# Attention with memory and a gated feed-forward: first statistics, last inverses and last adds moved between engines

## The chip, the cores and the metric

The kernel runs on one core of a Trainium2 chip. The metric is device time in microseconds from the launch to the end of the program on that core. The kernel before takes 261.97 us (median of 3 runs, 261.74 to 262.56). Its profiled execution spans 260.2 us from the first instruction to the last; all times inside the kernel below are counted from the start of that span.

The engines go by short names in the profile: PE is TensorE (matmul), PEld its weight load, DVE is VectorE, ACT is ScalarE, POOL is GpSimd, SP is SyncE, which here only issues transfers.

## The reference

The input is 2048 rows of 448 numbers in bfloat16. The rows are normalised, and then go through two branches, whose results are multiplied and added to the input. Cut to what matters:

```python
xn = layernorm(x)                       # (x - mean) / sqrt(var + 1e-5)
# branch A: 16 heads of 28, four segments of 512 rows
for s in range(4):
    p = softmax(q_s @ k_s.T * scale + causal_mask)
    a_dot = p @ v_s
    a_mem = (phi(q_s) @ M) / (phi(q_s) @ z + 1e-6)
    o_s = g * a_mem + (1 - g) * a_dot   # g = sigmoid(beta), one per head
    M, z = M + phi(k_s).T @ v_s, z + phi(k_s).sum(rows)
A = concat(o) @ wo
# branch B
B = (gelu(xn @ w_gate) * (xn @ w_up)) @ w_down
out = x + A * silu(B)
```

## The kernel before

A segment is 512 rows in NB = 4 blocks of 128; the 16 heads stand in G = 4 groups of HG = 4 heads, each head padded from 28 to 32 columns, so that a group fills 128 partitions. Column 28 of each padded head of v holds ones, so the softmax denominators come out of the same matmuls as the products. Attention of a segment is ten steps, and all other work (projections, down projections, memory reads, inverses, output projections) is placed between those steps by one table of step numbers.

The start: block statistics are shared between VectorE (blocks 0 and 1) and ScalarE (blocks 2 and 3).

```python
for i in range(44):                                     # L116: keeps TensorE busy while x loads
    nc.tensor.matmul(out=idle[:, 0:P], lhsT=wz[:], rhs=wz[:], start=True, stop=True)
w_dma(nc.sync, wv_sb, A_wv)
w_dma(nc.scalar, wk_raw, A_wk)
w_dma(nc.sync, wq_raw, A_wq)
...
def stats(b):                                           # L288 to L295, VectorE and a power on GpSimd
    nc.vector.bn_stats(out=st[:], in_=xs[:, b, :])
    nc.vector.bn_aggr(out=mv[:, b, :], in_=st[:])
    ... # rstd = (var + EPS) ** -0.5; tensor_scalar on vector, pow on gpsimd
def scale_x(b):                                         # L301, L304
    nc.vector.tensor_scalar(out=xn[b][:, 0:D], ...)     # (x - mean) * rstd
    nc.vector.tensor_scalar(out=xn[b][:, D:], ...)      # last 64 columns once more
def turn(b, copy=nc.scalar.copy):                       # L315, L316: four transposes, one copy out
    for c in range(NDC):
        nc.tensor.transpose(tp[:, c, :], xn[b][:, c * P:(c + 1) * P], ident[:])
    copy(out=dst, in_=tp[:])
def stats_scalar(b):                                    # L321 to L323
    nc.scalar.activation(out=junk[:], in_=xs[:, b, :], func=ACT.Copy, accum_out=mv[:, b, 0:1])
    nc.scalar.activation(out=mv[:, b, 0:1], in_=mv[:, b, 0:1], func=ACT.Copy, scale=-1.0 / D)
    nc.scalar.activation(out=junk[:], in_=xs[:, b, :], func=ACT.Square, bias=mv[:, b, 0:1],
                         accum_out=mv[:, b, 1:2])

def layer_norm_first():
    ...
    for b in (2, 3): stats_scalar(b)
    for b in (0, 1): stats(b)
    for b in (2, 3): power_scalar(b)                    # L329, L331 on gpsimd
    more_loads()                                        # w_gate, w_up, beta, next x, w_down: all on sync
    for b in (0, 1): scale_x(b)
    turn(0, nc.vector.tensor_copy)
    turn(1)
    for b in (2, 3): scale_x(b)
    pad_weight("wk")                                    # L144, vector
    for i in range(2):                                  # L358, L359
        nc.gpsimd.memset(vaug[i][:, :, :, Dh:HP], 0.0)
        nc.gpsimd.memset(vaug[i][:, :, :, Dh:Dh + 1], 1.0)
    for b in range(NB):
        run(units0[8 + b:9 + b])                        # value projection of a block, L431, L433
        if b < 2: turn(b + 2)
    pad_weight("wq")                                    # L144, scalar
# then eight projections of keys and queries (L392), then the first gate phase
```

GpSimd fills `spread`, the matrix that spreads inverses over partitions, with one memset and three affine selects (L188, L191); these wait for nothing.

The end: the denominators of the attention product go by DMA to a tile with 64 numbers in a row (`dc`), are inverted there, split into three bfloat16 terms, and go by DMA to `rows`; a matmul with `spread` brings them to all partitions. The last group of the last segment takes another way, by float32 matmuls:

```python
def invert(s, side, g0=0, g1=G, ...):                   # L541 to L549
    nc.vector.tensor_scalar(out=d, in0=d, ...)          # add 1e-6 or 0, times gate
    nc.vector.reciprocal(out=d, in_=d)
    for i in range(3):
        eng.tensor_copy(out=t[p, i, :], in_=d)
        if i < 2: eng.tensor_tensor(out=d, in0=d, in1=t[p, i, :], op=ALU.subtract)
        queues[i].dma_start(out=rows[...], in_=t[p, i, :])
def inverses(s, side, g, at):                           # L560
    nc.tensor.matmul(out=r[:], lhsT=spread[:, g, :], rhs=rows[at][:], start=True, stop=True)
def invert_last():                                      # L571 to L580
    for b in range(NB):
        nc.tensor.matmul(out=d[:, b, :], lhsT=o_a[:, b * P:(b + 1) * P], rhs=pick[:], ...)
    nc.vector.reciprocal(out=lden[:], in_=d[:])
    for h in range(2):
        nc.vector.tensor_tensor(out=linv[...], in0=lden[...], in1=lgate[...], op=ALU.mult)
def combine_last():                                     # L586 to L590
    for b in range(NB):
        nc.tensor.matmul(out=r[:, b * P:(b + 1) * P], lhsT=linv[:, b, :], rhs=unit[:], ...)
    for h in range(2):
        nc.vector.tensor_tensor(out=oT[3][:, G - 1, c], in0=o_a[:, c], in1=r[:, c], op=ALU.mult)
def combine(s, g, at=0):                                # L613, L614
    nc.vector.tensor_tensor(out=o_a, in0=o_a, in1=r, op=ALU.mult)
    add.tensor_tensor(out=dst, in0=o_a, in1=oU.pop((s, g, 1)), op=ALU.add)
...
combine_last()
srcs = [(om[0], G - 1)] + [(oT[3][:, g, :], g) for g in range(G)]     # memory part of group 3 apart
for b, a, z in ((0, 0, G), (1, 0, G), (0, G, G + 1), (1, G, G + 1), (2, 0, G + 1), (3, 0, G + 1)):
    for n in range(a, z): ...                           # L921: output matmuls, block by block
for b in range(NB):
    nc.vector.tensor_tensor(out=t, in0=t, in1=acc[...], op=ALU.mult)            # L926
    add = nc.gpsimd if b < 3 else nc.vector
    add.tensor_tensor(out=o_out[:, b, :], in0=t, in1=xr[3][:, b, :], op=ALU.add) # L928
    (nc.scalar if b % 2 else nc.sync).dma_start(out=o_v[3][:, b, :], ...)
```

In the same stretch stand the last down projections (L653 on TensorE, L659 on ScalarE, L663 on VectorE) and the output projections of segment 2 (L688, L691, L696).

Of the kernel before, what the change touches and what calls it, by code (L numbers as in the profile page):

```python
# [48 lines left out]
def fast_path(tc, A_x, A_wq, A_wk, A_wv, A_wo, A_beta, B_w_gate, B_w_up, B_w_down, out):  # L49
# [16 lines left out]
    with ExitStack() as ctx:  # L66
# [49 lines left out]
        for i in range(44):  # L116
            nc.tensor.matmul(out=idle[:, 0:P], lhsT=wz[:], rhs=wz[:], start=True, stop=True)
# [13 lines left out]
        for t in (wq_raw, wk_raw, wv_sb):  # L131
            nc.vector.memset(t[DR:P, NDC - 1, :], 0.0)
        w_dma(nc.sync, wv_sb, A_wv)
        w_dma(nc.scalar, wk_raw, A_wk)
        w_dma(nc.sync, wq_raw, A_wq)
# [23 lines left out]
        pick = const.tile([P, HG], F32, name="pick")  # L159
        unit = const.tile([P, P], F32, name="unit")  # L160
        lgate = const.tile([P, HG], F32, name="lgate")
        betal = const.tile([P, HG], A_beta.dtype, name="betal")

        def more_loads():
            w_dma(nc.sync, wg_sb, B_w_gate)
            n = (NDC - 1) * P
            nc.sync.dma_start(out=wu_sb[:], in_=B_w_up[0:n, :].rearrange("(c p) n -> p c n", p=P))
            nc.sync.dma_start(out=wg_sb[DR:P, NDC - 1, :], in_=B_w_up[n:D, :])
            nc.sync.dma_start(
                out=betac[:],  # L170
                in_=A_beta.rearrange("(h o) -> h o", o=1).unsqueeze(1).to_broadcast([H, RC, 1]))
            nc.sync.dma_start(
                out=betal[:],
                in_=A_beta[H - HG:H].rearrange("(o h) -> o h", o=1).to_broadcast([P, HG]))
            load_x(1)
            nc.sync.dma_start(out=wd_sb[:], in_=B_w_down.rearrange("(c p) n -> p c n", p=P))
# [7 lines left out]
        def fill_masks():  # L184
# [9 lines left out]
            for t, w, m in ((pick, -HP, -Dh), (unit, -1, 0)):  # L194
                nc.gpsimd.memset(t[:], 0.0)
                nc.gpsimd.affine_select(out=t[:], in_=t[:], pattern=[[w, t.shape[1]]],
                                        compare_op=ALU.not_equal, fill=1.0, base=m,
                                        channel_multiplier=1)
# [5 lines left out]
        def gates():  # L204

            nc.scalar.activation(out=igate[:, 0:1], in_=betac[:], func=ACT.Exp)
            nc.scalar.activation(out=igate[:, 1:2], in_=betac[:], func=ACT.Exp, scale=-1.0)
            nc.scalar.activation(out=lgate[:], in_=betal[:], func=ACT.Exp)
            for t in (igate, lgate):
                nc.vector.tensor_scalar(out=t[:], in0=t[:], scalar1=1.0, scalar2=2.0,  # L210
                                        op0=ALU.add, op1=ALU.mult)
            nc.vector.reciprocal(out=lgate[:], in_=lgate[:])
# [34 lines left out]
        def guard():  # L247
# [14 lines left out]
            nrm = const.tile([1, 2, H], F32, name="nrm")  # L262
# [6 lines left out]
            okh = const.tile([1, H], F32, name="okh")  # L269
# [8 lines left out]
        def layer_norm(s):  # L278
# [7 lines left out]
            def stats(b):  # L286
# [3 lines left out]
                if s == 0 or b % 2:  # L290
                    r = slice(b - (s > 0), b + 1)
                    r, v = rstd[:, r], mv[:, r, 1]
                    nc.vector.tensor_scalar(out=r, in0=v, scalar1=EPS,  # L293
                                            scalar2=None, op0=ALU.add)
                    nc.gpsimd.tensor_tensor(out=r, in0=r, in1=nhalf[:, 0:r.shape[1]], op=ALU.pow)  # L295

            def scale_x(b):
                xn[b] = xns[b]

                minus = ALU.add if b in scalar_mean else ALU.subtract  # L300
                nc.vector.tensor_scalar(out=xn[b][:, 0:D], in0=xs[:, b, :], scalar1=mv[:, b, 0:1],  # L301
                                        scalar2=rstd[:, b:b + 1], op0=minus, op1=ALU.mult)
# [3 lines left out]
                                        op0=minus, op1=ALU.mult)  # L306

            def turn(b, copy=nc.scalar.copy):
# [7 lines left out]
                copy(out=dst, in_=tp[:])  # L316

            def stats_scalar(b):

                junk = work.tile([P, D], BF16, name="ph_e")  # L320
                nc.scalar.activation(out=junk[:], in_=xs[:, b, :], func=ACT.Copy, accum_out=mv[:, b, 0:1])  # L321
                nc.scalar.activation(out=mv[:, b, 0:1], in_=mv[:, b, 0:1], func=ACT.Copy, scale=-1.0 / D)
                nc.scalar.activation(out=junk[:], in_=xs[:, b, :], func=ACT.Square, bias=mv[:, b, 0:1],  # L323
                                     accum_out=mv[:, b, 1:2])
                scalar_mean.add(b)

            def power_scalar(b):
                r = rstd[:, b:b + 1]
                nc.gpsimd.tensor_scalar(out=r, in0=mv[:, b, 1:2], scalar1=1.0 / D, scalar2=EPS,  # L329
                                        op0=ALU.mult, op1=ALU.add)  # L330
                nc.gpsimd.tensor_tensor(out=r, in0=r, in1=nhalf[:, 0:1], op=ALU.pow)  # L331

            scalar_mean = set()
            return (stats, scale_x, turn) if s else (stats, stats_scalar, power_scalar, scale_x, turn)

        def layer_norm_first():

            stats, stats_scalar, power_scalar, scale_x, turn = layer_norm(0)
            pad_columns("wq")
            pad_columns("wk")  # L340
            units0.extend(project_units(0))
            work = {2: [], 3: []}
            for b in (2, 3):
                stats_scalar(b)
            for b in (0, 1):
                stats(b)
            for b in (2, 3):
                power_scalar(b)
            more_loads()
            for b in (0, 1):  # L350
                scale_x(b)
            turn(0, nc.vector.tensor_copy)
            turn(1)
            for b in (2, 3):
                scale_x(b)
            pad_weight("wk")
            for i in range(2):
                nc.gpsimd.memset(vaug[i][:, :, :, Dh:HP], 0.0)  # L358
                nc.gpsimd.memset(vaug[i][:, :, :, Dh:Dh + 1], 1.0)  # L359
            for b in range(NB):  # L360
                run(units0[8 + b:9 + b])
                if b < 2:
                    turn(b + 2)
            pad_weight("wq")
# [144 lines left out]
        def evac(s, g, side, ps, copy=None):  # L509
# [6 lines left out]
            if (s, g, side) == (NSEG - 1, G - 1, 0):  # L516
                return
# [45 lines left out]
        lden = const.tile([P, NB, HG], F32, name="lden")  # L563

        om = []

        def invert_last():

            o_a, d = oU[NSEG - 1, G - 1, 0], ps_m.tile([P, NB, HG], F32, name="m")
            for b in range(NB):  # L570
                nc.tensor.matmul(out=d[:, b, :], lhsT=o_a[:, b * P:(b + 1) * P], rhs=pick[:],  # L571
                                 start=True, stop=True)
            nc.vector.reciprocal(out=lden[:], in_=d[:])
            for h in range(2):
                b = slice(h * NB // 2, (h + 1) * NB // 2)
                dims = [P, NB // 2, HG, HP]
                nc.vector.tensor_tensor(
                    out=linv[:, b, :].rearrange("p b (i d) -> p b i d", d=HP),
                    in0=lden[:, b, :].unsqueeze(3).to_broadcast(dims),
                    in1=lgate[:].unsqueeze(1).unsqueeze(3).to_broadcast(dims), op=ALU.mult)  # L580

        def combine_last():

            o_a, r = oU.pop((NSEG - 1, G - 1, 0)), ps_m.tile([P, L], F32, name="m")
            for b in range(NB):
                nc.tensor.matmul(out=r[:, b * P:(b + 1) * P],  # L586
                                 lhsT=linv[:, b, :], rhs=unit[:], start=True, stop=True)
            for h in range(2):
                c = slice(h * L // 2, (h + 1) * L // 2)
                nc.vector.tensor_tensor(out=oT[NSEG - 1][:, G - 1, c], in0=o_a[:, c], in1=r[:, c],  # L590
                                        op=ALU.mult)

        def scale_memory(s, g):
            o_n = oU[s, g, 1]
            done.add(("scl", s, g))

            if (s, g) == (NSEG - 1, G - 1):
                om.append(const.tile([P, L], BF16, name="mbd"))
            dst = om[0][:] if (s, g) == (NSEG - 1, G - 1) else o_n
            nc.vector.tensor_tensor(out=dst, in0=o_n, in1=inverses(s, 1, g, 1), op=ALU.mult)  # L600
# [230 lines left out]
        def follow(s, ends):  # L831
# [7 lines left out]
            else:  # L839
                put(f"inv{s}", lambda: invert(s, 0, 0, G - 1, **quick))  # L840
                put(f"inv{s}l", invert_last)
# [46 lines left out]
        linv = const.tile([P, NB, P], F32, name="macc")  # L888
# [26 lines left out]
        combine_last()  # L915

        srcs = [(om[0], G - 1)] + [(oT[3][:, g, :], g) for g in range(G)]
        for b, a, z in ((0, 0, G), (1, 0, G), (0, G, G + 1), (1, G, G + 1), (2, 0, G + 1), (3, 0, G + 1)):
            for n in range(a, z):
                src, g = srcs[n]  # L920
                nc.tensor.matmul(out=acc[b // 2][:, b % 2, 0:D], lhsT=src[:, b * P:(b + 1) * P],  # L921
                                 rhs=wo_sb[:, g, :], start=(n == 0), stop=(n == G))
# [390 lines left out]
```

## Time and profile before

| what | value |
|---|---|
| time, median of 3 | 261.97 us |
| span of the profiled execution | 260.2 us |
| first x landed (first bn_stats) | 4.12 us |
| first projection of keys | 12.18 us |
| last add ends (L928 on VectorE) | 254.04 us |

The page gives each engine's busy time and its share of the span, and a chain of work: followed back from the last instruction, at each step to what released it. A timeline has one instruction or a merged run of equal ones in a line: start in us, duration in us, engine, line of the kernel, operation, output<-inputs, shapes, count, and in brackets how long the engine was idle before it and what ended that. A duration includes what an instruction waited inside its engine. Consecutive instructions of an engine overlap a little, so steps from start to start are shorter than durations.

### The profile page before, as it was taken

The numbers are of one execution on the slowest core, as the hardware profiler recorded it, in microseconds if no ns is written. First come the engines' busy times: TensorE is split into PE (matmuls) and PEld (weight loads), VectorE is DVE, ScalarE is ACT, GpSimd is POOL, SyncE is SP. The second block draws the span as 40 slices with busy tenths as digits, with TensorE's granted clock in tenths as the row PEclk, the third lists the DMA queues.
The fourth block names the chain that finished last, engine by engine and source line by source line (L and its number), as shares of the span: only waits on it lengthen the run. The fifth ranks groups of instructions, "written<-read, shape, count | busy, mean of one in ns | idle before, by whom it ended". The sixth has DMA issues, their size and how long they took to land.

```text
span 260.2 us, 4481 instructions
## 1 busy us (share of the span) xinstructions
PE 243.5 (94%) x1609; PEld 102.7 (39%) x1609; DVE 187.5 (72%) x373; ACT 157.3 (60%) x220; POOL 93.0 (36%) x196
## 2 busy tenths in 40 slices
PE   6899999999999999999999998999999999999960
PEld 6443334343333334443443332343333333335530
DVE  5876687737996698798665796364699866778970
ACT  5656474689985326689873333433598788884100
POOL 2810163344632120555520344013064554572040
PEclk9999999999999999999999999999999999999995
DMA  7999205201120116021110021000200010001111
GB/s 217 345 326 254 30 0 126 72 0 24 27 39 9 25 29 158 27 58 24 39 40 0 17 53 24 4 0 8 73 19 21 25 26 4 10 4 25 53 33 50
DMA packets 27509, 15.07 MB, mean 58 GB/s; under 512 B 17880, under 2 KB 26584, under 8 KB 27480
## 3 DMA queue, kind: packets, MB, share of 16 engines
q1 hardware_dynamic: 25276, 12.93, 20.3%
q10 hardware_dynamic: 2204, 1.79, 2.3%
q8 instruction: 14, 0.23, 0.4%
q14 instruction: 15, 0.12, 0.1%
HBM read 9.18 MB, written 1.84 MB: 42 GB/s over the span
## 4 chain that ended last, share of the span: by engine, by line
PE 71%; DVE 12%; ACT 6%; DMA 3%; issue 2%; POOL 1%; ACTq 0%; DVEq 0%
PE s L627 23%; PE m L653 13%; PE m L392 10%; PE s L634 5%; PE s L483 5%; PE pv L502 4%; PE m L431 3%; PE m L688 3%; ACT pt L489 2%; DVE hT L643 2%; PE m L560 2%; PE s L921 1%; DMA pkb<-pqT 1%; ACT gl L642 1%; DMA x_sb<-in_A_x_dram 1%
## 5 line engine op out<-in xcount | busy, mean ns | idle before, releaser
L489 ACT ACTIVATE pt<-s 128x1024 bf16<-128x1024 f32 x80 | 77.5, 1023 | 13.1 <-PE s L483 9.9
L493 POOL TENSOR_SCALAR_AFFINE_SELECT pt<-pt 128x256 bf16<-128x256 bf16 x128 | 56.5, 462 | 66.3 <-ACT pt L489 63.4
L642 ACT ACTIVATE gl<-s 128x512 bf16<-128x512 f32 x56 | 33.4, 597 | 56.5 <-PE s L627 30.8
L643 DVE TENSOR_TENSOR hT<-gl,s 128x512 bf16<-128x512 bf16 x56 | 38.2, 684 | 31.6 <-ACT gl L642 31.6
L653 PE MATMUL m<-wd_sb,hT 128*128 128x448 bf16 x224 | 50.2, 353 | 0.0
L627 PE MATMUL s<-xnT,wg_sb 128*128 128x512 bf16 x168 | 45.7, 381 | 1.1 <-DVE hT L643 1.0
L627 PE MATMUL s<-xnT,wu_sb 128*128 128x512 bf16 x168 | 45.4, 379 | 0.0
L653 PEld LDWEIGHTS <-hT 128*128 128x128 bf16 x224 | 20.6, 98 | 21.4 <-issue 3.0
L627 PEld LDWEIGHTS <-wu_sb 128*128 128x128 bf16 x168 | 16.4, 98 | 19.8
L627 PEld LDWEIGHTS <-wg_sb 128*128 128x128 bf16 x168 | 13.9, 98 | 22.2 <-issue 10.1
L634 PE MATMUL s<-xnT,wg_sb 64*128 64x512 bf16 x112 | 19.6, 384 | 1.7 <-DVE hT L643 1.7
L295 POOL TENSOR_TENSOR rstd<-rstd,nhalf 128x2 f32<-128x2 f32 (+1 forms) x8 | 5.4, 676 | 41.8 <-DVE rstd L293 41.8
L483 PE MATMUL s<-qT,kT 32*128 32x512 bf16 (+3 forms) x256 | 19.1, 300 | 1.1 <-ACT pt L489 0.5
L392 PE MATMUL m<-xnT,wq_pad 128*128 128x512 bf16 x64 | 17.5, 380 | 0.0
L392 PE MATMUL m<-xnT,wk_pad 128*128 128x512 bf16 x64 | 16.5, 380 | 0.2 <-DVE qT L396 0.2
L396 DVE CAST kT<-m 128x512 bf16<-128x512 f32 x16 | 11.0, 688 | 7.6 <-PE m L392 7.3
L502 PE MATMUL pv<-pt,vaug 128*32 128x128 bf16 (+3 forms) x256 | 15.9, 305 | 0.0
L431 PE MATMUL m<-wv_sb,xnT 128*128 128x448 bf16 x64 | 14.6, 353 | 1.2 <-DVE vaug L433 1.1
L659 ACT ACTIVATE th<-m 128x448 f32<-128x448 f32 x16 | 8.8, 548 | 9.6 <-PE m L653 9.6
L483 PEld LDWEIGHTS <-kT 32*128 32x128 bf16 x256 | 5.5, 91 | 18.5 <-issue 18.2
L634 PEld LDWEIGHTS <-wg_sb 64*128 64x128 bf16 x112 | 5.2, 93 | 19.1 <-issue 18.5
L546 POOL CAST terms<-dc 128x64 bf16<-128x64 f32 x12 | 3.0, 249 | 24.5 <-DVE dc L543 24.0
(130 smaller groups left out, 311.2 us busy)
## 6 DMA issues: line engine op xcount, KB each, us to landing
x_sb<-in_A_x_dram SPq DMA_DIRECT2D x7, 224.0 KB
wd_sb<-in_B_w_down_dram SPq DMA_DIRECT2D x1, 1568.0 KB
wg_sb<-in_B_w_gate_dram SPq DMA_DIRECT2D x1, 1344.0 KB
wu_sb<-in_B_w_up_dram SPq DMA_DIRECT2D x1, 1344.0 KB
xr<-in_A_x_dram ACTq DMA_DIRECT2D x2, 448.0 KB
out_dram<-o_out SPq DMA_DIRECT2D x8, 112.0 KB
out_dram<-wq_pad SPq DMA_DIRECT2D x4, 112.0 KB
wo_sb<-in_A_wo_dram SPq DMA_DIRECT2D x4, 98.0 KB
```

Source lines behind the costliest of these rows:

```text
L392: nc.tensor.matmul(out=pr[:], lhsT=wpad[nm][:, c, g * HG:(g + 1) * HG, :].rearrange("p h d -> p (h d)"), rhs=xnT[s][:, c, :], start=(c == ...
L396: (nc.scalar.copy if s == 0 and nm == "wq" else nc.vector.tensor_copy)(out=dst[:, g, :], in_=pr[:])
L431: nc.tensor.matmul(out=vp[:, 0:D], lhsT=xnT[s][:, c, b * P:(b + 1) * P], rhs=wv_sb[:, c, :], start=(c == 0), stop=(c == NDC - 1))
L483: nc.tensor.matmul(out=sp[i // 2][:, i % 2, c0:c0 + n], lhsT=kT[s][r, g, kb * P:(kb + 1) * P], rhs=qT[s][r, g, kb * P:L], start=True, stop ...
L489: nc.scalar.activation(out=pt[:, :, 0:w], in_=sp[pr][:, :, 0:w], func=ACT.Exp, scale=scale)
L493: nc.gpsimd.affine_select(out=v, in_=v, pattern=[[0, 2], [1, P]], compare_op=ALU.is_ge, fill=0.0, base=0, channel_multiplier=-1)
L502: nc.tensor.matmul(out=acc[i * HP:(i + 1) * HP, kb * P:L], lhsT=vaug[s % 2][:, kb, g * HG + i, :], rhs=pts[i // 2][:, i % 2, c0:c0 + n], s ...
L627: nc.tensor.matmul(out=gu[:, i, :], lhsT=w_sb[:, c, cols], rhs=xnT[s][:, c, :], start=start and c == 0, stop=stop and c == NDC - 2)
L634: nc.tensor.matmul(out=gu[:, i, :], lhsT=wg_sb[rs, NDC - 1, cols], rhs=xnT[s][rs, NDC - 1, :], start=start, stop=stop)
L642: nc.scalar.activation(out=gl[:], in_=gu[:, 0, :], func=ACT.Gelu_apprx_tanh)
L643: nc.vector.tensor_tensor(out=hT[s][:, fc, :], in0=gl[:], in1=gu[:, 1, :], op=ALU.mult)
L653: nc.tensor.matmul(out=d_ps[:, 0:D], lhsT=hT[s][:, fc, b * P:(b + 1) * P], rhs=wd_sb[:, fc, :], start=(fc == 0), stop=(fc == NFC - 1))
```

## The change

The changed kernel does the first statistics on VectorE alone, transposes all four blocks and only then projects values; the value tiles are cleared by VectorE. w_q is loaded ahead of w_v, and w_up through ScalarE's queue instead of SyncE's. It warms TensorE with 78 matmuls instead of 44. At the end the last group's inverses go through the same DMA path as the others (`rows[1]` holds them), the output matmuls run group by group with the last group last, and the last adds alternate between GpSimd and VectorE. The constants `pick`, `unit`, `lgate` go. It is for one uniform way of inverting and normalising, with GpSimd relieved of two of its chores. The diff, cut to its core (small renamings and removed helper definitions left out, cuts marked):

```diff
-        for i in range(44):
+        for i in range(78):
             nc.tensor.matmul(out=idle[:, 0:P], lhsT=wz[:], rhs=wz[:], start=True, stop=True)
...
+        w_dma(nc.sync, wq_raw, A_wq)
+        w_dma(nc.scalar, wk_raw, A_wk)
         w_dma(nc.sync, wv_sb, A_wv)
-        w_dma(nc.scalar, wk_raw, A_wk)
-        w_dma(nc.sync, wq_raw, A_wq)
...  # more_loads()
-            nc.sync.dma_start(out=wu_sb[:], in_=B_w_up[0:n, :]...)
-            nc.sync.dma_start(out=wg_sb[DR:P, NDC - 1, :], in_=B_w_up[n:D, :])
+            nc.scalar.dma_start(out=wu_sb[:], in_=B_w_up[0:n, :]...)
+            nc.scalar.dma_start(out=wg_sb[DR:P, NDC - 1, :], in_=B_w_up[n:D, :])
...  # gates()
-            nc.scalar.activation(out=lgate[:], in_=betal[:], func=ACT.Exp)
-            for t in (igate, lgate):
-                nc.vector.tensor_scalar(out=t[:], in0=t[:], scalar1=1.0, scalar2=2.0, ...)
-            nc.vector.reciprocal(out=lgate[:], in_=lgate[:])
+            nc.vector.tensor_scalar(out=igate[:], in0=igate[:], scalar1=1.0, scalar2=2.0, ...)
...  # stats(b): one power for two blocks, in segment 0 too
-                if s == 0 or b % 2:
+                if b % 2:
...  # layer_norm_first()
-            for b in (2, 3):
-                stats_scalar(b)
-            for b in (0, 1):
-                stats(b)
-            for b in (2, 3):
-                power_scalar(b)
+            for b in range(3):
+                stats(b)
             more_loads()
-            ...  # as shown above
+            pad_weight("wq")
+            scale_x(0)
+            turn(0)
+            stats(3)
+            for b in range(1, NB):
+                scale_x(b)
+                turn(b)
+            for i in range(2):
+                nc.vector.memset(vaug[i][:, :, :, Dh:HP], 0.0)
+                nc.vector.memset(vaug[i][:, :, :, Dh:Dh + 1], 1.0)
+            pad_weight("wk")
+            units0.extend(project_units(0))
+            run(units0[8:])
...  # the last inverses
-                put(f"inv{s}l", invert_last)
+                put(f"inv{s}l", lambda: invert(s, 0, G - 1, G, 1, **quick))
...  # the end
-        combine_last()
-        srcs = ...
+        for g in range(G - 1):
+            wo_part(g)                  # four matmuls, one for each block
+        combine(3, G - 1, 1)
+        wo_part(G - 1)
...
-            add = nc.gpsimd if b < 3 else nc.vector
+            add = nc.vector if b % 2 else nc.gpsimd
```

## The prediction

> **What bounds the kernel now.** I read the share of busy time first, then the chain of work that ended last, and then, because the change touches only the first 13 us and the last 25, the timelines of those two stretches.
>
> ```profile
> PE 243.5 (94%) x1609; PEld 102.7 (39%) x1609; DVE 187.5 (72%) x373; ACT 157.3 (60%) x220; POOL 93.0 (36%) x196
> PE 71%; DVE 12%; ACT 6%; DMA 3%; issue 2%; POOL 1%; ACTq 0%; DVEq 0%
> ```
>
> TensorE is busy nearly throughout and carries 71% of the chain, so whatever delays its first useful matmul is carried through to the end: there is almost no idle time in which to catch up. The chain in order of time shows what holds it back at the start.
>
> ```profile
> 4.42 0.68 ACT ph_e L321 x2
> ...
> 8.08 0.56 POOL rstd L331
> ...
> 8.98 0.65 DVE xn L304
> 9.63 0.47 DVE wk_pad L144
> 10.09 0.54 DVE vaug L433
> 10.63 0.04 issue
> 10.67 1.67 PE m L431 x8
> ```
>
> The first x lands at 4.1 to 4.4, statistics and scaling take until 9.63, and the value projection (L431) ends at 12.2, when the projection of keys begins (first L392 at 12.18 in the timeline). At the end it is VectorE that matters:
>
> ```profile
> 239.79 0.25 DVE L573 RECIPROCAL lden<-m 128x16 f32<-128x16 f32 x1
> 240.07 0.76 DVE L577 TENSOR_TENSOR macc<-lden,lgate 128x256 f32<-128x256 f32 x2
> 240.75 0.61 DVE L691 TENSOR_TENSOR sg<-sg,m 128x448 f32<-128x448 f32 x1
> ...
> 248.53 0.74 DVE L590 TENSOR_TENSOR oT<-oU,m 128x256 bf16<-128x256 f32 x2
> 249.83 1.15 DVE L926 TENSOR_TENSOR wg_sb<-wg_sb,s 128x448 f32<-128x448 f32 x2 [0.56 <-PE s L921]
> 251.72 1.15 DVE L926 TENSOR_TENSOR wg_sb<-wg_sb,s 128x448 f32<-128x448 f32 x2 [0.74 <-PE s L921]
> 252.91 1.13 DVE L928 TENSOR_TENSOR wv_sb<-wg_sb,x_sb 128x448 bf16<-128x448 f32 x1
> ```
>
> From 238.7 to 249.3 VectorE has no idle entry at all, although the chain names TensorE (PE is equally full, 4.00 of every 4 us from 240 to 248). Work added to VectorE here is added to the end. The last add ends at 254.04; output transfers and the end of the program fill the remaining 6.2 us and don't change.
>
> [...]
>
> ```profile
> 35.01 1.88 POOL L258 TENSOR_TENSOR pqT<-pqT 128x896 bf16<-128x896 bf16 x1
> 36.36 0.67 DVE L301 TENSOR_SCALAR xn<-x_sb,mv,rstd 128x448 bf16<-128x448 bf16 x1
> 36.95 1.10 DVE L304 TENSOR_SCALAR xn<-x_sb,mv,rstd 128x64 bf16<-128x64 bf16 x1
> 36.97 1.04 POOL L260 TENSOR_TENSOR pqT<-pqT 128x448 bf16<-128x448 bf16 x1
> ```
>
> L301 (0.39 undisturbed) ends 0.14 after L258 does (36.89), then L260 gets in, and L304 (0.29 undisturbed) ends 0.04 after L260 (38.01): the engines take turns. The last DVE L928 is the same case: 1.13 instead of the 0.62 that the same shape takes at L696, ending 0.49 after a GpSimd add that ran from 252.52 to 253.55. [...] Here 21 warming matmuls take 2.15 us at first (0.102 each) and the last five 0.32 (0.064 each). [...] the 8 KB transfer of denominators takes 1.70 here (the chain at 234.97).
>
> **The change, part by part.** The order of instructions on each engine is the same in both programs from the first projection of keys to step 139, apart from three gate operations and the buffer of one product. So I price start, gates and end.
>
> *Start.* Removed: ScalarE's statistics of blocks 2 and 3, and the interleaving of value projections with transposes. VectorE now does four sets. Steps from start to start in the timeline: bn_stats to aggregate 0.66, to tensor_scalar 0.22, to the next instruction 0.07 (0.09 where no tensor_scalar stands between). From 4.12: block 0's statistics to 4.87, block 1's with the shared tensor_scalar to 5.81; block 2's to 6.55. GpSimd's power of two columns (0.70) ends at 6.67 and costs 0.2 more to reach VectorE: block 0 is scaled from 6.86 (0.30 and 0.21), block 3's statistics run 7.37 to 8.31, block 1 is scaled to 8.9, and the second power ends at about 9.2.
>
> Here comes the part that I count as a new cost. Before, GpSimd's clearing of the value tiles and of the spread matrix came behind the last powers, with only one block left to scale. Now nothing but the second power stands ahead of the spread matrix: one memset (about 0.5, an estimate from 0.20 for 128 columns and 0.31 for 256) and three affine selects (0.73 each) start at 9.25, just before VectorE wants to scale blocks 2 and 3 in four instructions. If they take turns as above: memset to 9.8, first scale to 9.9, select to 10.6, then 10.65, select to 11.35, 11.5, select to 12.2, last scale 12.25. Without the lock it would be 10.4. Transposes of block 3 end 0.42 later (9.63 to 10.05 before), at 12.67, and only then do sixteen value matmuls run, at 0.19 each (before: 8 in 1.5): 3.0, to 15.6. Meanwhile VectorE clears the value tiles (four memsets, about 0.45 from 0.17 and shorter) and pads wk (0.47): done at 13.3, hidden. ScalarE pads wq (1.69) before its first copy: wq should land by 6 to 7 (1.26 MB wanted by then, at the 0.33 to 0.38 MB per us of the windows), so the first copy is ready near 8.5: hidden. So keys start at 15.6 instead of 12.18: **+3.4**; without the lock 13.7: +1.5. The 34 extra warming matmuls end near 7.9 (34 at 0.06 behind 5.84), before they hold up anything. But TensorE is then left with 16 short transposes for over 4 us, so the clock may fall; 14 matmuls in 2.6 us at half rate would lose 1.3, and I put 40% on it: **+0.5**.
>
> *Gates.* One exponential, one tensor_scalar and one reciprocal go. VectorE's last value copy there started at 46.45 behind them and TensorE waited 0.47 for it: **-0.3**. Loads of w_up on another queue move the same bytes: 0.
>
> *End.* VectorE loses L573 and L577 (239.79 to 240.75: 0.96) and gains seven instructions of the DMA path on 32x64: the same seven on 96x64 took 236.79 to 238.73, 1.94 from start to start, and rows don't count (L543 takes 0.55 on 128 rows and on 96). The evacuation ends at 237.87, so its denominators (1.70 plus 0.05) are in by 239.7, before VectorE asks at 239.9: no wait. So the next L691 starts at 241.9 instead of 240.75, **+1.1**; the thirteen operations from it on, 7.8 us to L590's place, end at 249.7. TensorE gains little from the sixteen float32 matmuls that go (about 0.9 each eight): its buffers come free through VectorE. The rows of inverses leave at 241.8 and need about 2: hidden. Then: four output matmuls of group 2 and the spreading matmul (0.75 and 0.4) behind oT of group 2 at 249.3, to 250.4; combine 0.70 and 0.69 to 251.8 (before: 0.74); four matmuls for group 3, the first block ready at 252.1. Before, the fourth block's matmuls ended near 251.7, so this part adds little for the last blocks, but all four multiplications now stand behind it: m0, m1 to 253.2; add 1 on VectorE, held by GpSimd's add 0 (252.7 to 253.7) and 0.49 after it, to 254.2; m2, m3; add 3 held by add 2 (254.7 to 255.75) to 256.2. Against 254.04: **+2.2** for the whole end, of which about 0.5 is the second contended add.
>
> Sum: 3.4 + 0.5 - 0.3 + 2.2 = 5.8. I choose 4.9, as 20% stands for the case without the lock (1.9 less, or 0.4), and as a late start lets the initial loads and the first transposes by DMA finish sooner against the work (0.5, a choice): 261.97 + 4.9 = **266.9 us**.
>
> **Rivals.** First: no lock at the start (GpSimd's selects slip behind VectorE's burst). For it: L415 in attention is never over 0.45 beside many selects, 0.28 alone. Against: each clear case shows turns. It gives 264.5 to 265.5. Second: the inverses' rows by DMA arrive late and the end waits for them. For it: two transfers of 1.7 to 2 us with 2 us of VectorE between. Against: they are wanted at 250.0 and ready near 244. It would give 268 or more. Third: the old start was bound by ScalarE (L321 to L323 are on the chain), so unloading it gains. Against: VectorE needs 0.95 per block where the two engines shared four blocks. It would give 264. Fourth: the float32 matmuls removed shorten a TensorE-bound end, since the chain names them (L586 0.89); VectorE's full stretch speaks against it; it would make the end 0.5 to 1 longer only, near 265.5.
>
> **Range and chances.** Low end: no lock, end +1.5: 265.2 with rounding upward of the rest. High end: lock, slow clock, contended adds: 268.9. The 2% line lies at 267.2, just above my number: 1% faster, 54% within, 45% slower.
>
> **What would show it.** Keys' first projection at 15.6 (13.7 without the lock); long scale operations (over 0.6) for blocks 2 and 3, next to spread's selects; value matmuls at 0.19, or 0.37 if the clock fell; seven 32x64 operations on VectorE and the next L691 1.1 later, counted from the delay of the start; no wait on the last rows; two VectorE adds near 1.1. Wrong if blocks 2 and 3 scale in 0.4, if wq lands after 8.5, or if VectorE shows idle time between 240 and 249.

## The result, and the profile after

The changed kernel takes 265.39 us (median of 4, 265.22 to 266.45) against 262.18 us for the kernel before in the same session: a ratio of 1.0132, interval 1.0100 to 1.0163. It is slower, but by less than 2%. The profiled execution is the longest of the four, 266.45 us with a span of 264.7 us; what sets it apart is TensorE's clock (0.979 on average against 0.984 to 0.987 in the other three), which fell at the start; the experiments below take this up.

The shares of busy time and the chain by engine, from the page of the changed kernel:

```profile
PE 244.9 (93%) x1624; PEld 102.5 (39%) x1624; DVE 192.3 (73%) x383; ACT 154.5 (58%) x210; POOL 88.8 (34%) x183
PE 71%; DVE 16%; ACT 5%; issue 2%; DMA 2%; POOL 1%; POOLq 0%
```

These two lines can't show where the loss is. TensorE's share of the chain is the same 71%. VectorE's went from 12 to 16% and its busy time from 187.5 to 192.3 us; ScalarE and GpSimd lost 2.8 and 4.2 us of work. That is what the edit says and not yet a reason. The chain in order of time shows the start (start us, us, what):

```profile
8.80 0.56 DVE xn L282
9.36 0.71 DVE xn L285
10.07 0.28 DVE xn L282
10.36 0.63 DVE xn L285
10.99 0.05 issue
11.03 0.23 PE m L296
11.26 4.71 PE m L387 x16
15.97 6.92 PE m L348 x32
```

L282 and L285 scale a block: 0.39 and 0.29 where nothing disturbs them, here 0.56, 0.71, 0.28 and 0.63 in the chain's shares. They run beside GpSimd's filling of the spread matrix:

```profile
8.71 0.52 POOL L180 MEMSET spread<- 128x512 bf16 x1
9.30 2.43 POOL L183 TENSOR_SCALAR_AFFINE_SELECT spread<-spread 128x512 bf16<-128x512 bf16 x3
```

Then the sixteen value matmuls (L387) take 4.71 us instead of about 3.0. The first projection of keys comes at 15.81 in the timeline, 3.63 later than before. VectorE's timeline shows the end:

```profile
241.88 0.61 DVE L583 SCALAR_TENSOR_TENSOR wg_sb<-th,m 128x448 f32<-128x448 f32 x1
242.52 0.25 DVE L495 TENSOR_SCALAR dc<-dc,igate 32x64 f32<-32x64 f32 x1
242.81 0.55 DVE L497 RECIPROCAL dc<-dc 32x64 f32<-32x64 f32 x1
...
244.57 0.62 DVE L611 TENSOR_TENSOR sg<-sg,m 128x448 f32<-128x448 f32 x1
...
253.80 0.69 DVE L534 TENSOR_TENSOR oT<-oU,wu_sb 128x512 bf16<-128x512 f32 x1
255.13 1.15 DVE L846 TENSOR_TENSOR wg_sb<-wg_sb,s 128x448 f32<-128x448 f32 x2 [0.65 <-PE s L836]
256.32 1.03 DVE L848 TENSOR_TENSOR wv_sb<-wg_sb,x_sb 128x448 bf16<-128x448 f32 x1
257.27 1.14 DVE L846 TENSOR_TENSOR wg_sb<-wg_sb,s 128x448 f32<-128x448 f32 x2
258.45 1.02 DVE L848 TENSOR_TENSOR wv_sb<-wg_sb,x_sb 128x448 bf16<-128x448 f32 x1
```

L495 begins right behind the operation before it, so the last denominators were there in time. Seven operations on 32x64 fill 242.52 to 244.57, and L611, which is L691 of the kernel before, starts 3.82 later than there. The last add ends at 259.47 instead of 254.04.

Where the difference arose is read by subtracting the start of each instruction from that of its twin in the kernel before. The third column does the same for the changed kernel with idle matmuls (the second run with fillers below), in whose profiled execution TensorE's clock stayed up.

| stretch | predicted | changed, profiled | clock up |
|---|---|---|---|
| first projection of keys | +3.4 +0.5 -0.4 | +3.63 | +2.14 |
| first transposes by DMA, 27 to 32 us | -0.5 | -0.51 | -0.52 |
| first gate phase, 44 to 49 us | -0.3 | -0.29 | -0.29 |
| another gate phase, near 160 us | 0 | -0.23 | -0.23 |
| end, last evacuation to last add | +2.2 | +2.83 | +2.83 |
| last add to end of span | 0 | -0.93 | -0.63 |
| sum | +4.9 | +4.50 | +3.30 |

The first x landed 0.37 us earlier in the profiled execution than in that of the kernel before (3.75 against 4.12), and 0.17 earlier in that of the third column (3.95). Counted from x, the start therefore costs 4.00 with the fall of the clock and 2.31 without. Of the delay 0.5 was given back by 32 us, the gate phases saved another 0.5, and the end then added its own.

### The profile page after: what moved, and what is told of

It reads as the page before. It is cut to its first block, busy times and chain, and to the rows that moved or that the text cites. A ratio compares the mean times of both kernels' runs of the same rounds, so it can differ in the third digit from the quotient of the medians.

```text
span 264.7 us, 4500 instructions
## 1 busy us (share of the span) xinstructions
PE 244.9 (93%) x1624; PEld 102.5 (39%) x1624; DVE 192.3 (73%) x383; ACT 154.5 (58%) x210; POOL 88.8 (34%) x183
## 4 chain that ended last, share of the span: by engine, by line
PE 71%; DVE 16%; ACT 5%; issue 2%; DMA 2%; POOL 1%; POOLq 0%
PE s L547 25%; PE m L573 12%; PE m L348 10%; PE s L554 6%; PE s L439 4%; PE m L387 4%; PE pv L458 4%; PE m L608 2%; ACT pt L445 2%; DVE hT L563 2%; DVE oU L533 2%; PE m L514 2%; DVE xn L285 1%; DVE oT L534 1%; ACT gl L562 1%
## 5 line engine op out<-in xcount | busy, mean ns | idle before, releaser
L573 PE MATMUL m<-wd_sb,hT 128*128 128x448 bf16 x224 | 50.2, 353 | 0.0
L573 PEld LDWEIGHTS <-hT 128*128 128x128 bf16 x224 | 20.6, 98 | 22.2 <-issue 3.9
L278 POOL TENSOR_TENSOR rstd<-rstd,nhalf 128x2 f32<-128x2 f32 x8 | 5.8, 728 | 49.0 <-DVE rstd L276 49.0
L387 PE MATMUL m<-wv_sb,xnT 128*128 128x448 bf16 x64 | 15.9, 386 | 0.2 <-DVE vaug L389 0.2
L608 PE MATMUL m<-wo_sb,oT 128*128 128x448 bf16 x48 | 11.4, 353 | 0.4 <-DVE sg L611 0.2
```

What stands on the lines that cost most here:

```text
L387: nc.tensor.matmul(out=vp[:, 0:D], lhsT=xnT[s][:, c, b * P:(b + 1) * P], rhs=wv_sb[:, c, :], start=(c == 0), stop=(c == NDC - 1))
L573: nc.tensor.matmul(out=d_ps[:, 0:D], lhsT=hT[s][:, fc, b * P:(b + 1) * P], rhs=wd_sb[:, fc, :], start=(fc == 0), stop=(fc == NFC - 1))
L608: nc.tensor.matmul(out=a_ps[:, 0:D], lhsT=oT[s][:, g, b * P:(b + 1) * P], rhs=wo_sb[:, g, :], start=(g == 0), stop=(g == G - 1))
```

## Experiments

**Start alone and end alone.** Theory: the two are separate costs. The first kernel is the one before with the changed start, the second the changed kernel with the start of before.

```diff
# start only                              # end only
-  stats_scalar(2), stats_scalar(3)       +  stats_scalar(2), stats_scalar(3)
+  stats(b) on VectorE, b = 0 to 3        -  stats(b) on VectorE, b = 0 to 3
-  range(44)                              +  range(44)
+  range(78), w_q first, w_up by ScalarE  -  range(78), w_q first, w_up by ScalarE
   last inverses and adds as before          last inverses and adds as changed
```

> The changed start with the end of the kernel before. My theory: the changed program is late by three separate amounts, start +3.6 us in the profiled run, of which about 0.8 is given back by 165 us (the first transposes by DMA, a wait in the third gate phase), and the end. Without the changed end it should take 264.3 to 265.0, and its first projection of keys should begin near 15.8, or near 14.2 in executions in which the TensorE clock does not fall. Rival (the loss is in the end, and the start's delay is absorbed by the work that follows): 262 to 262.8.

> The start of the kernel before with the changed end (and without the three gate operations). My theory: +2.8 us from the last evacuation to the last add, -0.3 at the gates, up to -0.9 from output transfers that are issued further apart: 263.5 to 264.7. Rival (the float32 matmuls that go shorten the end, TensorE bound): 261.0 to 262.5.

Measured: the start alone 263.58 us, ratio 1.0075 [1.0049, 1.0100], less than the 264.3 to 265.0 that I expected; the end alone 264.16 us, ratio 1.0107 [1.0082, 1.0132]. In the profile of the first, keys come 2.40 later; 1.89 of it is left at 32 us and arrives whole at the last add. In the second the end, from last evacuation to last add, takes 2.85 longer. So both halves cost, and they add roughly: 2.1 and 2.7 us by the medians make 4.7, against 4.1 for the changed kernel with the clock up (265.6 against 261.5, by the two runs with fillers below). Of the 0.6 between, 0.27 is a delay near 226 us that only the profile of the end alone has; the rest stays unexplained.

**Spread matrix filled earlier.** Theory: the long scales come from GpSimd's fills beside them. The fills go where GpSimd has nothing to do, ahead of the powers.

```diff
 def layer_norm_first():
+    fill_spread()            # memset and three affine selects on GpSimd
     pad_columns("wq")
...
 def fill_masks():
-    # the same memset and selects
```

> The changed kernel, but GpSimd fills the spread matrix while x is still loading, ahead of the first power, instead of beside the scaling of blocks 2 and 3. [...] the four scale operations of blocks 2 and 3 take 0.39 and 0.29 instead of 0.56, 0.79, 0.38 and 0.70; the last one ends about 1.1 earlier, near 9.9, and the time falls by 1.0 to 1.2 (more, up to 2.5, if the clock then holds). Rival (the long scale operations come from something else, as the loads or the power): no change of those durations, time within 0.3 of the changed kernel.

Measured: 264.66 us, ratio 1.0126 [1.0101, 1.0151], 263.71 for the profiled execution. Its chain at the same place:

```profile
9.33 0.40 DVE xn L284
9.72 0.21 DVE xn L287
9.94 0.31 DVE xn L284
10.25 0.05 issue
10.30 0.44 PE m L298 x4
10.73 3.03 PE m L390 x16
```

The scales are back at their own length (0.40, 0.30, 0.39 and 0.29 in the timeline). As the landing of x moves between executions (3.75 to 4.37), I count keys from it: 10.38 after x in the kernel with the start alone, 9.31 here, 8.06 in the kernel before. The fills beside the scales cost **1.07 us**, and the rest of the rearranged start 1.25, which no run took apart.

**Idle matmuls between the transposes.** Theory: the sixteen value matmuls were slow because TensorE's clock fell after a stretch with little work.

```diff
 scale_x(0); turn(0)
+keep_busy(8)                 # 8 matmuls 128x128 into an unused bank
 stats(3)
 for b in range(1, NB):
     scale_x(b); turn(b)
+    keep_busy((10, 6, 0)[b - 1])
```

> The changed kernel with 24 more idle matmuls of 128 columns (8, 10 and 6) in the gaps between the transposes of the four blocks, so that TensorE is busy there. Theory of the clock: it fell to half near 11.3 because TensorE had little to do from 7.5 to 11; with the fillers the 16 value matmuls take 0.19 each instead of 0.37, keys begin near 14.1 instead of 15.8, and the time is 1.2 to 1.8 below a changed execution in which the clock fell. Rival (the clock falls for another reason, or the value matmuls are slowed by their buffers): no change, or the fillers delay the transposes by some 0.3.

> The changed kernel itself once more, beside the next three, as their measure, since chips and executions differ by some tenths. Expected 1.012 to 1.017 of the kernel before, with keys at about 10.4 us after x lands if the TensorE clock holds and 12 if it falls: if both kinds occur, the clock is a matter of the execution and not of the program.

Measured: with fillers 265.57 us, ratio 1.0159 [1.0134, 1.0183], four executions from 265.39 to 265.75. The changed kernel again, on another chip: 266.50 us, ratio 1.0176 [1.0145, 1.0207], two executions at 265.7 and 265.8 and two at 267.2 and 267.5. This settles nothing, because on the chip of the fillers the clock had stayed up without them too (0.988 to 0.994 in the kernel with the start alone). So both ran once more, on one chip.

> The changed kernel with 24 idle matmuls between its transposes, once more with more executions. Theory that the fall of TensorE's clock at 11 to 15 us comes of TensorE's scarce work there, and that keeping it at work prevents it: every execution between 265.2 and 266.1, none at 267. Rival that the clock falls in some executions whatever stands there: a fourth to a half of the executions 1.5 to 2 us above the rest, as in the changed kernel.

> The changed kernel once more, on the same chip as the run with idle matmuls. Theory: a fourth to a half of its executions about 1.7 us above the rest (267.3 against 265.7), the rest no different from the kernel with idle matmuls. Rival, that the two populations belong to a chip or an hour: all executions alike.

Measured: with fillers 265.51 us, ratio 1.0164 [1.0150, 1.0178], all five executions from 265.26 to 266.02. Without: 267.44 us, ratio 1.0227 [1.0206, 1.0248], four of five at 267.4 to 267.9, more than the fourth to a half that I expected. The windows of one microsecond, for TensorE alone, of the changed kernel's first profile and then of the second one with fillers (window, length, PE busy, granted clock, DMA share, GB/s):

```profile
11.00:12.00 1.00, 0.97 (x4) 0.64 1.02 405
12.00:13.00 1.00, 1.00 (x4) 0.50 1.04 412
```

```profile
11.00:12.00 1.00, 0.83 (x7) 1.00 1.10 425
12.00:13.00 1.00, 1.00 (x8) 1.00 0.98 387
```

Half the clock and half the matmuls in the same microsecond.

In the changed kernel's first profile the clock fell near 11.3 and stayed at 0.50 for about 3.4 us; ahead of that TensorE had little work. Its busy time in the three microseconds from 8 to 11, for two profiles with a fall and five of the changed start without one (the granted clock is that of the microsecond from 12):

| profile | from 8 | from 9 | from 10 | sum | clock |
|---|---|---|---|---|---|
| changed, first | 0.44 | 0.34 | 0.57 | 1.35 | 0.50 |
| changed, again | 0.36 | 0.29 | 0.57 | 1.22 | 0.50 |
| last inverses on GpSimd | 0.81 | 0.29 | 0.57 | 1.67 | 1.00 |
| start alone | 1.00 | 0.29 | 0.57 | 1.86 | 1.00 |
| float32 matmuls kept | 1.00 | 0.29 | 0.57 | 1.86 | 1.00 |
| with fillers, first | 0.43 | 0.88 | 0.59 | 1.90 | 1.00 |
| spread matrix earlier | 0.80 | 0.46 | 0.93 | 2.19 | 1.00 |

The third profile with a fall has 0.29 and 0.57 from 9. The starts of the kernel with the start alone, with the last inverses on GpSimd and with the float32 matmuls have no fillers and no fall in these profiles; there the warming matmuls end later, and 15 to 19 matmuls stand in the microsecond from 8 instead of 4 in the two with a fall. The fillers add work from 9 on, 0.88 instead of 0.29 to 0.34. What decides which execution falls, these runs don't show beyond this.

With the fillers the clock stayed up in all nine executions (0.983 to 0.987 on average), but they don't shorten anything else: keys come 10.37 after x with them, just as in an execution of the changed kernel's start whose clock stayed up by itself. Over its three runs the changed kernel had a mean clock of 0.979 or less in 7 of 13 executions; these average 267.36 us, the other six 265.66.

**The last inverses on GpSimd.** Theory: VectorE's queue sets the end of the changed kernel, so five of its seven new operations taken off it bring their length back.

```diff
-put(f"inv{s}l", lambda: invert(s, 0, G - 1, G, 1, **quick))
+put(f"inv{s}l", lambda: invert(s, 0, G - 1, G, 1, eng=nc.gpsimd, queues=quick["queues"]))
```

> The changed kernel with the five small casts and subtractions of the last inverse on GpSimd instead of VectorE (the sum with 1e-6 and the reciprocal stay). Theory (VectorE is the bound of the end): 5 times 0.24 = 1.2 us leave its queue, everything behind moves up, time 0.8 to 1.2 lower than the changed kernel on the same chip. Rival (the inverses' transfers, later by some 0.3 on GpSimd, or TensorE set the end): no change or 0.3 longer.

Measured: 265.35 us, ratio 1.0147 [1.0103, 1.0191]; the four executions (264.17 to 266.62) spread too widely to show a gain of 1 us, and one of them has the mean clock of a fall, 0.979. The end by itself is clear in the profile: 1.81 us longer than before instead of 2.83. VectorE's timeline:

```profile
241.62 0.55 DVE L497 RECIPROCAL dc<-dc 32x64 f32<-32x64 f32 x1
242.19 0.62 DVE L611 TENSOR_TENSOR sg<-sg,m 128x448 f32<-128x448 f32 x1
```

L611 follows the reciprocal at once. In the changed kernel the five operations had taken 1.18 (243.39 to 244.57), and 1.02 came back.

**Float32 matmuls kept.** Rival: TensorE bounds the end, and eight float32 matmuls less had shortened it.

```diff
+for b in range(NB):
+    nc.tensor.matmul(out=d[:, b, :], lhsT=oU[s, G - 1, 0][:, b * P:(b + 1) * P], rhs=nhalf[:], ...)
 invert(s, 0, G - 1, G, 1, **quick)
```

> The changed kernel with the eight float32 weight loads and matmuls of the kernel before put back at the step of the last inverse; their result is read by nobody, so this only adds TensorE work of 0.95 us and the use of one buffer. Theory (the chain named TensorE but VectorE sets the pace there): 0 to 0.3 longer than the changed kernel. Rival (TensorE bound): 0.9 longer.

Measured: 266.75 us, ratio 1.0207 [1.0168, 1.0247], again two and two executions (265.6 to 265.8, 267.7). The profiled one has its end 2.85 longer than before; without them it was 2.83. They took 0.95 us of TensorE's time and cost nothing here: TensorE has to wait for VectorE a little later anyway, before the first spreading matmul, 1.19 us without them and 0.53 with them. These are the eight of the last inverses; the other eight that the change removes (L586, which the chain before names) were not put back.

**Both repairs at once.**

```diff
+    fill_spread()            # ahead of the powers
-put(f"inv{s}l", lambda: invert(s, 0, G - 1, G, 1, **quick))
+put(f"inv{s}l", lambda: invert(s, 0, G - 1, G, 1, eng=nc.gpsimd, queues=quick["queues"]))
```

> The changed kernel with two repairs at once: GpSimd fills the spreading matrix before it works out the powers, so that no fill runs beside the block scales, and the last inverse's five casts and subtractions run on GpSimd. Theory that the two costs are separate terms of one sum: against the changed kernel 1.0 us at the start where TensorE's clock holds and 1.0 at the end, so about 263.5 us and a ratio of 1.007 to 1.009 where the clock holds; the end part, last evacuation to last store, longer than before's by 1.8. Rival that the gains overlap (a start that is earlier meets the loads again, 0.3 to 0.5 us of wait at 30 us): 264.0 us, ratio 1.010. Both stay above the kernel before, because the rest of the start (statistics all on VectorE, one more pair of powers) and the split additions stay.

Measured: 263.49 us, ratio 1.0076 [1.0059, 1.0092], on the chip where the changed kernel took 267.44 and the one with fillers 265.51. Keys come 9.31 after x and the end is 1.80 longer than before. Each repair brings what it brought alone: 2.0 us together against the kernel with fillers, whose clock stays up as here (0.982 to 0.985).

**Towards a faster kernel.** Two edits of the kernel before. The first moves GpSimd's fills ahead of the powers there, gives block 3's statistics to VectorE and both first copies to ScalarE.

```diff
+    # vaug's memsets and fill_spread() on GpSimd, ahead of the powers
-    stats_scalar(2), stats_scalar(3), stats(0), stats(1), power_scalar(2), power_scalar(3)
+    stats_scalar(2), stats(0), stats(1), power_scalar(2), stats(3)
-    turn(0, nc.vector.tensor_copy)
+    turn(0)
```

> The kernel before with a start drawn from these findings: GpSimd fills spread and the value tiles while x loads, block 3's statistics go to VectorE and only block 2's to ScalarE, both transposed blocks are copied by ScalarE. Theory: no scale operation is blocked (0.39 and 0.29), scaling ends about 0.6 earlier, keys begin about 7.2 to 7.6 after x lands instead of 8.1, time 0.4 to 0.8 below the kernel before. Rival (the powers on GpSimd come late behind the fills, or loads set the start): equal or slower.

Measured: 261.43 us, ratio 0.9999 [0.9988, 1.0010]: a miss. The last scale ended 5.06 after x instead of 5.51, yet keys came 8.09 after x, as before (8.06). GpSimd's fills ended only at 5.67 and delayed the first power to 5.64. The first copy was therefore ready at 8.31, and from there TensorE had its 3.0 us of value matmuls and its transposes to do in any order.

The second takes the same five operations off VectorE, in the inverses of groups 0 to 2.

```diff
-put(f"inv{s}", lambda: invert(s, 0, 0, G - 1, **quick))
+put(f"inv{s}", lambda: invert(s, 0, 0, G - 1, eng=nc.gpsimd, queues=quick["queues"]))
```

> The kernel before with one edit: the five casts and subtractions of the last segment's inverses of the groups 0 to 2 (96x64) run on GpSimd and no longer on VectorE. Theory that VectorE's queue is the bound of the end in the kernel before too: the addition behind them (line 691) moves from 238.73 to about 237.7, VectorE keeps the order behind it, and the last store leaves 0.7 to 1.0 us earlier; median 260.5 to 260.8, ratio 0.996 to 0.997. Rival: the rows of the groups 0 to 2 come later from GpSimd (its five operations took 2.27 us against 1.15 on VectorE in the changed kernel with that edit), the first spreading matmul (242.04 before) waits for their transfer, and half or all of it is given back: ratio 0.998 to 1.001. Rival that TensorE's matmuls bound this end (it stands behind line 928 with 0.56 and 0.74 of VectorE's idle time): ratio 0.999 to 1.001.

Measured: 261.27 us against 261.50, ratio 0.9988 [0.9977, 0.9999], where I had expected 260.5 to 260.8. It is the fastest version here, by a hair. VectorE's timeline says why it is no more:

```profile
236.93 0.55 DVE L543 RECIPROCAL dc<-dc 96x64 f32<-96x64 f32 x1
238.37 0.62 DVE L691 TENSOR_TENSOR sg<-sg,m 128x448 f32<-128x448 f32 x1 [0.89 <-PE m L688]
```

The time set free became a wait for TensorE. L691 starts 0.36 earlier than before, of which 0.14 was there ahead of the edit (L541 at 236.65 against 236.79).

## Why the prediction was right, and where it wasn't

**Start, +3.4: the kind was right, the size wasn't.** What the prediction calls the lock is my reading of three VectorE operations in the trace of the kernel before (0.67, 1.10 and 1.13 us instead of 0.39, 0.29 and 0.62 beside GpSimd's) as turns of the two engines; what lies behind them wasn't shown. I estimated strict turns of scale and select: four scales ended by 12.25, and 1.85 us lost. The last scale ended at 10.98, 7.23 after x where I had 8.13, and the fills beside the scales cost 1.07. The four scales took 0.56, 0.79, 0.38 and 0.70 in the timeline. The two longest end just behind a select: the first two selects end at 10.03 and 10.94, the scales beside them at 10.07 and 10.98. But the third scale waited for nothing, and it was the second select that took longer (0.83 instead of 0.73). So it isn't one select between every two scales. My mark, over 0.6 for blocks 2 and 3, was passed by only two of the four. The case without turns was placed well: keys 9.58 after x predicted (at 13.7), 9.31 measured with the fills moved away. The chance of 20% given to it (-0.4) stood for a case that didn't come.

**Clock, +0.5: both terms were too small, and the median hid it.** That the clock might fall, and for 2.6 us, was my estimate. A fall costs 1.7 us and not 1.3, because it lasted 3.4 us: keys come 12.06 after x with the fall, 10.37 without, and 1.70 between the two averages above. It came in 7 of 13 executions, not in 40%, which makes 0.9 on average. In the first comparison the clock fell in one execution of four, so the median 265.39 has nothing of it; in the last one it fell in four of five, and the median is 267.44. The same kernel is 1.3% or 2.3% slower by the number of falls that a comparison catches, so that the median came below my number and not above it is chance. With the clock up the start costs 2.14 where my terms for it sum to 3.5, and this is the largest part of the difference between 266.9 and 265.39. With the clock down it costs 3.63, and that this is near 3.5 is luck: turns priced too high and a fall priced too low cancel in part, and x landed 0.37 earlier. The 3.4 us are from the granted clocks: 0.64, 0.50, 0.50 and 0.65 in the four microseconds from 11 make 0.72 + 1 + 1 + 0.70 = 3.42 us at half the clock. The two other profiled falls give 3.40 (from 0.61, 0.50, 0.50, 0.69) and 3.42 (from 0.83, 0.50, 0.50, 0.50, 0.96). Of the executions that were not profiled only the mean clock is known.

**The late start absorbed, -0.5: right, though a choice.** Before, ScalarE waited at 27.75 us for the transposes by DMA (a step of 3.78 us in the chain), idle for 0.74. A later start finds them done. The start alone shows it too: 2.40 shrinks to 1.89.

**Gates, -0.3: right** (-0.29). That another -0.23 would come near 160 us I didn't foresee. The end alone shows it too (-0.24) and the start alone doesn't, so it came with that half of the edit and not with the late start; what in that half brings it is open.

**End, +2.2: the first step exact, the tail too short.** The seven operations take 2.05 from start to start (242.52 to 244.57) where L573 and L577 took 0.96: +1.09, predicted +1.1. VectorE has no idle time up to 251.75 plus its 0.61, as predicted, and the combine ends at 251.9 in unshifted time (251.8 predicted). Then the first multiplication starts at 252.5, not 252.1: blocks 0 and 1 lie in one accumulator tile, and it waits for the matmuls of both. The multiplications and contended adds take 4.34, not 4.1. Together about +0.65.

**"Work added to VectorE here is added to the end": true, but not its inverse.** In the changed kernel 1.18 us off VectorE brought 1.02. In the kernel before, 1.07 off VectorE brought some 0.2. There TensorE stood just behind VectorE as the bound, at L691, which waited 0.89 for L688's matmul once the five operations were gone; the seven added operations opened a gap between the two, and that gap is what could be won back. What work taken off VectorE behind that L691 would bring, no run shows.

**Last add to end of span, "don't change": it varied:** 5.6 to 6.3 us in the four profiled executions with the old order of the last stores, 4.7 to 6.0 in the ten with the new order. Part of the -0.93 may belong to that order; no run took it apart.

**Rivals.** No lock, that is no turns: fell with the scales (0.79 and 0.70 for 0.29) and the early fills (1.07 less). Late rows: a transfer of rows takes 2.25 in the chain of the changed kernel, and no wait on them appeared there. ScalarE unloaded gains: fell for the start as a whole, which even with the fills moved away is 1.25 longer; what the statistics taken off ScalarE do alone no run shows. Float32 matmuls shorten the end: it became 2.85 longer alone, not 0.5 to 1, and eight of the sixteen cost nothing when put back; the other eight weren't tried.

**The low end of the range was summed too high.** Its terms (start +1.5 without turns, gates -0.3, end +1.5) make 264.7, or 264.2 with the 0.5 for the late start, and not 265.2. The measured 265.39 lies just above the stated end.

## What to carry to other kernels

Before moving chores between engines, lay the helper's new place against what its neighbour runs in that microsecond: the same fill cost 1.07 us beside the block scales, and while x was still loading it left the scales at 0.40, 0.30, 0.39 and 0.29. Where two engines are nearly full, a queue that lengthens the end when work is added needn't shorten it when work is taken away, so test both directions. When a clock can fall, go by all executions and not only by the median of a few.

## What the hardware showed

The clock fell although TensorE was not idle: in the changed kernel it was busy 0.34 of the microsecond from 9 and 0.57 of the next, with transposes, and 78 warming matmuls had run before. With 24 matmuls that compute nothing the shares were 0.88 and 0.59 in one profile and 1.00 and 0.80 in the other, and the clock stayed up in all nine executions. In the eight executions with the early fills, whose keys come 1.07 us earlier, it stayed up as well (0.982 to 0.988 on average). But in the four of the kernel with the start alone it stayed up with the whole stretch, on another chip; only the last comparison, four falls of five against none of five on one chip, carries the verdict on the fillers by the times.
